# Score rounds and projection halves on 64x64 TensorE tiles, with PV rounds left on 64x32 tiles

## The chip, the cores and the metric

The kernel runs on one core of one Trainium2 chip. The metric is the device time of one execution in microseconds (us); lower is better. Five engines matter: TensorE (PE, with its weight loads listed apart as PEld), VectorE (DVE), ScalarE (ACT), GpSimd (POOL) and SyncE (SP), which issues most DMAs.

## The reference

The reference normalises `x` (2048 rows of 512), runs multi-query attention with 32 heads of width 16 that share one key head and one value head, runs a dense block with SiLU, and joins the two:

```python
xn = _layernorm(x)                                    # [2048, 512]
q = (xn @ wq) in 32 heads of 16;  k = xn @ wk;  v = xn @ wv
p = softmax(q k^T * 16 ** -0.5);  s = (p v) @ wo      # one k, one v for all heads
h = silu(xn @ w1);  g = silu(h @ w2)                  # 512 -> 1792 -> 512
out = x + s * g
```

All tensors are bf16; only `x`, the five weights and `out` are in HBM.

## The kernel before

**Work.** The 2048 queries are cut into 4 chunks of 512 columns, the 32 heads into groups of 4, which makes 32 groups (g) of a chunk and four heads. A *score round* multiplies 64 keys by the queries of two of a group's heads: its result fills one PSUM bank, 128 partitions (64 keys for each head) by 512 queries. There are 2048 score rounds. Their exponentials go two ways. ScalarE takes part of the banks with `Exp` into `pa_sb` (line 1570). VectorE takes the others with a scale and a cast to integers into `db_sb` (line 951), from which GpSimd makes shifted copies in `ds_sb` by integer additions (line 1136). A *PV round* then multiplies such a block by the values (16 value columns and 16 columns of weights that sum the denominator, so 32 wide) and adds it into the group's output bank (line 1214). The exponential that VectorE makes is used in four copies, so there are more PV products than score blocks; one PV round takes two blocks.

**Projections.** `product` (its matmuls are at line 644) cuts every 128-row step of four projections into two halves of 64 rows: `q` (from `wq`), `h` (from `w1`), `z` (from `w2`) and `w` (from `wo`). `tail_half` (its matmul is at line 1421) does the same with the last chunk's `wo` product. So nearly all of TensorE's work is in rounds whose contraction has 64 rows.

**Two lanes.** A matmul carries a tile size (rows by columns of TensorE's array) and a tile position. In the kernel before, score rounds, PV rounds and projection halves all use tiles of 64 rows by 32 columns, four to a round. A round of lane 0 uses the tiles at (0,0), (0,32), (64,64) and (64,96); a round of lane 1 those at (64,0), (64,32), (0,64) and (0,96). Score rounds are always on lane 1, PV rounds always on lane 0, projection halves on either. The rounds of the two lanes touch no tile in common.

**Order.** A planner in the kernel's Python writes the order of every engine's instructions before the program is built. It works with fixed durations: `MM` = 216 ns for one round on a lane, a latency between each two engines, and `SWITCH` = 105 ns when TensorE passes to a round of another mode letter. The letters are "U" for the 64-row rounds, "C" for 128 rows by 32 columns (lines 530, 572, 674), "H" for 128 by 64 (line 609) and "F" for 128 by 128 (lines 546, 1461, 1530). `Planner.tensor` keeps one clock per lane for "U". The order on TensorE is strict; a wait for a semaphore stands ahead of the instruction that needs it.

**Buffers.** Eight PSUM banks hold score blocks, PV outputs and projection results; the planner gives them out as they come free.

Of the kernel before, what the change touches and what calls it, by code (L numbers as in the profile page):

```python
# [15 lines left out]
P = 128  # L16
# [287 lines left out]
def bass_recurrent_scan__grouped_kv_mqa__dense_activation_silu__prompt_kernel(  # L304
# [27 lines left out]
    NQR, NON = 4, 2 * NOC  # L332

    with ExitStack() as es:
        def sb(name, shape, dt):
            return es.enter_context(nc.sbuf_tensor(name, shape, dt))
# [10 lines left out]
        kt_sb = sb("kt_sb", [P, 2, 2, S], BF16)  # L347
# [3 lines left out]
        qt_sb = sb("qt_sb", [P, NQR, NQ], BF16)  # L351
# [6 lines left out]
        on_sb = sb("on_sb", [P, NON, NQ], BF16)  # L358
# [26 lines left out]
        def bank(b):  # L385
            return ps[:, b * 512:(b + 1) * 512]
# [98 lines left out]
        first = (2, 2, 4, 4, 4)  # L485
        a = 0
        for n in first:
            b = a + n
            tiles = range(a, b)
            g = a // 4  # L490
            y, w, h = rstd_sb[:, a:b], var_sb[:, 0, a:b], var_sb[:, 1, a:b]
# [140 lines left out]
        def product(jb, lhs, rhs, needs):  # L632
            n = len(jb.rounds)
            jb.mode, jb.place, jb.rounds = "U", [0, 0], []
            jb.left = 2 * n

            def half(k, l):
                b, first, last = jb.bank, jb.left == 2 * n, jb.left == 1

                def emit(pe):  # L640
                    for j in range(4):
                        r0 = 64 * (j // 2 ^ l)
                        rows = slice(r0, r0 + 64)
                        h = pe.matmul(bank(b)[32 * j:32 * (j + 1), :], lhsT=lhs(k, rows, 32 * j, 32), rhs=rhs(k, rows),  # L644
                                      start=first, stop=last, tile_position=(r0, 32 * j), skip_group_check=True)
                    return h
                return emit
            jb.half, jb.needs, jb.n = half, needs, n
            return
# [220 lines left out]

        def s_half(b, g, i, kb):
            def emit(pe):
                for j in range(4):
                    r0, k0 = 64 * (j // 2 ^ 1), 64 * kb + 32 * (j % 2)
                    h = pe.matmul(bank(b)[32 * j:32 * j + 32, :], lhsT=kt_sb[r0:r0 + 64, g % 2, i, k0:k0 + 32],  # L875
                                  rhs=qt_sb[r0:r0 + 64, g // 2 % NQR, :], start=True, stop=True, tile_position=(r0, 32 * j),
                                  skip_group_check=True)
                return h
            return emit
# [498 lines left out]
        tb = []  # L1378
# [19 lines left out]
        def tail_reads(r, o):  # L1398
            oi = NOC * (NC - 1) + o
            return ["wo", ("on", oi % NON) if o < NOC - 1 else ("on", oi % NON, r // 2)]  # L1400

        def tail_half(l, t):
            if not tail["half"][l]:
                return INF
            r, o = tail["half"][l][0]
            oi = NOC * (NC - 1) + o
            if t2_task.get(oi) is None or t2_task[oi].op is None or tb[r] not in pool_free:
                return INF
            if l == 0 and any(q == r for q, _ in tail["half"][1]):
                return INF  # L1410
            rr = pl.ready(PE, tail_reads(r, o), [("ps", tb[r])] if o == 0 and l == 1 else ())
            if l == 0 and o == 0:
                rr = max(rr, pl.vis(tail["prev"][r], PE))
            if rr > t + 20:
                return rr
            tail["half"][l].pop(0)

            def emit(pe):
                for j in range(4):
                    r0 = 64 * (j // 2 ^ l)  # L1420
                    h = pe.matmul(bank(tb[r])[32 * j:32 * (j + 1), :],  # L1421
                                  lhsT=on_sb[r0:r0 + 64, oi % NON, r * P + 32 * j:r * P + 32 * (j + 1)],
                                  rhs=wo_sb[r0:r0 + 64, o, :], start=o == 0 and l == 1, stop=False,
                                  tile_position=(r0, 32 * j), skip_group_check=True)
                return h
            tail["prev"][r] = pl.tensor("U", l, MM, emit, tail_reads(r, o), [("ps", tb[r])], t,
                                        after=tail["prev"].get(r) if l == 0 and o == 0 else None)
            return True
# [171 lines left out]
        while True:  # L1600
            e = min(ENGINES, key=pl.clk.get)
            seen, r = quiet[e]
            if seen != pl.count or pl.clk[e] >= r:
                r = steps[e]()
# [73 lines left out]
```

## Time and profile before

| What | Value |
|---|---|
| median of two runs | 680.74 us (679.91 to 681.57) |
| the profiled execution: device time | 679.18 us |
| the profiled execution: span, first to last instruction | 677.4 us |
| granted TensorE clock, mean | 0.999 |
| busy: PE, ACT, DVE, POOL | 666.9, 658.7, 634.5, 606.3 us |
| TensorE matmuls, weight loads | 22037, 22038 |
| score rounds (line 875) | 8192 matmuls in 2048 rounds |
| PV rounds (line 1214) | 8800 matmuls |
| projection halves (line 644), tail halves (line 1421) | 4448 and 96 matmuls |

The time of an execution is 1.78 us more than its span. Matmuls are pipelined and the profile models their ends: a matmul of 512 columns has a duration of about 0.38 us, although another can start on the same tile 0.216 us after it. So the busy share of PE says little; the distance between the starts of two rounds says more. In a row of the timeline, "64*32 64x512" means a tile of 64 rows and 32 columns, and a moving operand of 64 partitions by 512 columns. Rows that follow each other on one engine with the same form are merged ("x4"); the times are the first start and the length from there to the last end.

### The profile page before, as it was taken

What the parts mean: (1) busy time and instruction counts of PE and PEld (TensorE: products, weight loads), DVE (VectorE), ACT (ScalarE), POOL (GpSimd) and SP (SyncE); (2) the same over time, 40 slices, a digit from 0 to 9 for tenths busy, and PEclk for the clock granted to TensorE, in tenths of its full rate; (3) what the DMA queues carried; (4) which work ended last, traced back from release to release, by engine and by line L of the source; (5) the groups of instructions that cost most, each with busy time, mean ns of one, the idle gap of its engine ahead of it and who ended that gap; (6) DMA issues with size and microseconds to landing.
All of it is one profiled execution on the core that took longest, in us unless ns stands there. A gap on an engine that the chain in (4) does not pass through costs nothing.

```text
span 677.4 us, 47302 instructions
## 1 busy us (share of the span) xinstructions
PE 666.9 (98%) x22037; PEld 362.0 (53%) x22038; DVE 634.5 (94%) x1150; ACT 658.7 (97%) x1194; POOL 606.3 (90%) x604
## 2 busy tenths in 40 slices
PE   8999999999999999999999999999999999999997
PEld 4445556555455545555655665555555565555542
DVE  8989999999999999999999999999999999999763
ACT  5899999999999999999999999999999999999996
POOL 4038998999999999989999997899999999998993
PEclk9999999999999999999999999999999999999999
DMA  8510000000000010000000100000000001000000
GB/s 298 170 30 4 4 5 5 4 5 4 5 4 20 21 35 5 4 4 5 5 4 4 36 21 20 5 5 5 4 5 4 20 21 35 4 6 4 5 4 33
DMA packets 11732, 14.98 MB, mean 22 GB/s; under 512 B 1808, under 2 KB 10768, under 8 KB 11536
## 3 DMA queue, kind: packets, MB, share of 16 engines
q1 hardware_dynamic: 10928, 10.78, 5.0%
q8 instruction: 172, 2.82, 1.8%
q0 software_dynamic: 320, 0.92, 0.5%
q10 hardware_dynamic: 288, 0.26, 0.1%
q14 instruction: 24, 0.20, 0.1%
HBM read 8.95 MB, written 2.10 MB: 16 GB/s over the span
## 4 chain that ended last, share of the span: by engine, by line
PE 87%; ACT 9%; DVE 2%; issue 1%
PE ps L875 40%; PE ps L1214 26%; PE ps L644 19%; ACT pa_sb L1570 9%; PE ps L1530 1%; PE ps L1421 0%; PE ps L572 0%; DVE kt_sb L590 0%; DVE stats_sb L478 0%; PE ps L546 0%; DVE xn_sb L507 0%; DVE v_sb L618 0%; DVE xnT_sb L557 0%; PE ps L609 0%; ACT t_sb L692 0%
## 5 line engine op out<-in xcount | busy, mean ns | idle before, releaser
L1570 ACT ACTIVATE pa_sb<-ps 128x512 bf16<-128x512 f32 (+1 forms) x1103 | 628.3, 759 | 7.4 <-PE ps L875 6.1
L1136 POOL INT64_ADD ds_sb<-db_sb x588 | 597.0, 1040 | 25.7 <-PE ps L1214 15.8
L875 PE MATMUL ps<-qt_sb,kt_sb 64*32 64x512 bf16 x8192 | 567.1, 379 | 2.8 <-issue 1.3
L951 DVE TENSOR_SCALAR db_sb<-ps 128x512 uint16<-128x512 f32 x784 | 493.0, 682 | 15.6 <-PE ps L875 12.2
L1214 PE MATMUL ps<-ds_sb,v_sb 64*32 64x512 bf16 x4704 | 410.0, 377 | 0.4 <-issue 0.3
L1214 PE MATMUL ps<-pa_sb,v_sb 64*32 64x512 bf16 x2528 | 317.6, 378 | 1.0 <-issue 0.4
L875 PEld LDWEIGHTS ps<-qt_sb,kt_sb 64*32 64x32 bf16 x8192 | 192.9, 90 | 204.4 <-ACT pa_sb L1570 111.3
L1214 PE MATMUL ps<-db_sb,v_sb 64*32 64x512 bf16 x1568 | 184.4, 377 | 0.0
L1214 PEld LDWEIGHTS ps<-ds_sb,v_sb 64*32 64x32 bf16 x4704 | 154.9, 91 | 22.9 <-issue 3.6
L644 PE MATMUL ps<-w_sb,u_sb 64*32 64x512 bf16 x1792 | 138.0, 377 | 0.1
L644 PE MATMUL ps<-xnT_sb,w_sb 64*32 64x512 bf16 x1792 | 136.7, 377 | 0.2
L1214 PEld LDWEIGHTS ps<-pa_sb,v_sb 64*32 64x32 bf16 x2528 | 93.8, 91 | 22.2 <-ACT pa_sb L1570 9.0
L1214 PEld LDWEIGHTS ps<-db_sb,v_sb 64*32 64x32 bf16 x1568 | 56.7, 91 | 7.7 <-issue 0.7
L644 PEld LDWEIGHTS ps<-xnT_sb,w_sb 64*32 64x32 bf16 x1792 | 44.0, 91 | 16.7 <-ACT pa_sb L1570 3.2
L644 PEld LDWEIGHTS ps<-w_sb,u_sb 64*32 64x32 bf16 x1792 | 45.1, 91 | 13.4 <-issue 1.2
L692 ACT ACTIVATE t_sb<-ps 128x512 bf16<-128x512 f32 x72 | 48.7, 676 | 0.0
L693 DVE SCALAR_TENSOR_TENSOR u_sb<-t_sb,ps 128x512 bf16<-128x512 bf16 x56 | 38.0, 679 | 1.8 <-ACT t_sb L692 1.3
L644 PE MATMUL ps<-xnT_sb,wq_sb 64*32 64x512 bf16 x480 | 37.2, 378 | 0.0
L1231 DVE STREAM_TRANSPOSE ps<-ps 128x512 f32<-128x512 f32 (+1 forms) x33 | 23.2, 706 | 12.9 <-PE ps L1214 12.9
L644 PE MATMUL ps<-wo_sb,on_sb 64*32 64x512 bf16 x384 | 29.3, 378 | 0.0
L1260 POOL DMA_DIRECT2D kt_sb<-kt_sb x4 | 2.8, 700 | 26.7 <-DVE mv_sb L482 18.1
L644 PEld LDWEIGHTS ps<-xnT_sb,wq_sb 64*32 64x32 bf16 x480 | 11.9, 91 | 5.6 <-ACT pa_sb L1570 1.0
(72 smaller groups left out, 182.9 us busy)
## 6 DMA issues: line engine op xcount, KB each, us to landing
w_sb<-in_B_w_dram SPq DMA_DIRECT2D x2, 1792.0 KB, 13.9
xr_sb<-in_A_x_dram SPq DMA_DIRECT2D x16, 128.0 KB, 3.3
out_dram<-ob_sb SPq DMA_DIRECT2D x16, 128.0 KB, 1.8
ds_sb<-in_A_x_dram SPq DMA_DIRECT2D x3, 512.0 KB, 7.2
kt_sb<-kt_sb POOLq DMA_DIRECT2D x4, 224.0 KB, 3.3
wq_sb<-in_A_wq_dram SPq DMA_DIRECT2D x1, 512.0 KB, 5.4
wo_sb<-in_A_wo_dram SPq DMA_DIRECT2D x1, 512.0 KB, 16.4
ds_sb<-in_A_x_dram ACTq DMA_DIRECT2D x2, 128.0 KB, 3.1
```

The lines of the kernel that those rows point to most:

```text
L644: h = pe.matmul(bank(b)[32 * j:32 * (j + 1), :], lhsT=lhs(k, rows, 32 * j, 32), rhs=rhs(k, rows), start=first, stop=last, tile_position=(r ...
L692: t1 = Task(AC, 477.0, lambda a: a.activation(t_sb[:, k, :], bank(b), ACT.Tanh, scale=scale), [("ps", b)], [("t", k)], 0)
L693: t2 = Task(DV, T_P, lambda v: v.scalar_tensor_tensor(out=dst, in0=t_sb[:, k, :], scalar=1.0, in1=bank(b), op0=ALU.add, op1=ALU.mult), [(" ...
L875: h = pe.matmul(bank(b)[32 * j:32 * j + 32, :], lhsT=kt_sb[r0:r0 + 64, g % 2, i, k0:k0 + 32], rhs=qt_sb[r0:r0 + 64, g // 2 % NQR, :], star ...
L951: bt.P[k] = pl.add(Task(DV, T_P, lambda v: v.tensor_scalar(db_sb[:, bt.b, k * NQ:(k + 1) * NQ], bank(b), 128.0 * LOG2E, 128.0 * (SHIFT_BET ...
L1136: whole["po"].append(pl.add(Task(PO, T_P64, lambda g: g.int64_add(ds_sb[:, s, :].bitcast(U64), db_sb[:, bt.b, :].bitcast(U64), words), rea ...
L1214: h = pe.matmul(bank(OB)[q:q + 32, :], lhsT=lhs[rows], rhs=rhs[rows], start=s0, stop=s1, tile_position=(64 * l, q), skip_group_check=True)
L1231: t1 = pl.add(Task(DV, (T_TR - 60.0) / parts + 60.0, lambda v, cols=cols: v.transpose(bank(OB)[:, cols], bank(OB)[:, cols]), [("ps", OB)], ...
L1260: kt1[c] = pl.add(Task(PO, T_SWDGE, lambda e: e.dma_start(kt_sb[DH:P, 1, :, cols], kt_sb[0:P - DH, 0, :, cols]), [("kt", k, a) for k in ra ...
L1530: pl.tensor("F", None, T_COLD if n <= N_COLD else MM, lambda pe: pe.matmul(bank(6), lhsT=zer_sb[:, 0:P], rhs=zer_sb[:, :], start=True, sto ...
L1570: op = pl.place(AC, 0.8333 * NQ * n + T_AF, lambda a: a.activation(pa_sb[:, s * NQ:(s + n) * NQ].rearrange("p (b n) -> p b n", n=NQ), ps3[ ...
```

## The change

In three places a loop of four matmuls on tiles of 64 rows by 32 columns becomes a loop of two on tiles of 64 by 64: the projection halves (`product`), the score rounds (`s_half`) and the halves of the last `wo` product (`tail_half`). The two tiles of lane 0 are then at (0,0) and (64,64), those of lane 1 at (64,0) and (0,64); each covers what two tiles of 64x32 covered. PV rounds (`do_pv`) keep four tiles of 64 by 32. Products, banks, operands and results are the same.

```diff
--- a projection half: product()
-                    for j in range(4):
-                        r0 = 64 * (j // 2 ^ l)
+                    for j in range(2):
+                        r0 = 64 * (j ^ l)
                         rows = slice(r0, r0 + 64)
-                        h = pe.matmul(bank(b)[32 * j:32 * (j + 1), :], lhsT=lhs(k, rows, 32 * j, 32), rhs=rhs(k, rows),
-                                      start=first, stop=last, tile_position=(r0, 32 * j), skip_group_check=True)
+                        h = pe.matmul(bank(b)[64 * j:64 * (j + 1), :], lhsT=lhs(k, rows, 64 * j, 64), rhs=rhs(k, rows),
+                                      start=first, stop=last, tile_position=(r0, 64 * j), skip_group_check=True)
--- a score round: s_half()
-                for j in range(4):
-                    r0, k0 = 64 * (j // 2 ^ 1), 64 * kb + 32 * (j % 2)
-                    h = pe.matmul(bank(b)[32 * j:32 * j + 32, :], lhsT=kt_sb[r0:r0 + 64, g % 2, i, k0:k0 + 32],
-                                  rhs=qt_sb[r0:r0 + 64, g // 2 % NQR, :], start=True, stop=True, tile_position=(r0, 32 * j),
+                for j in range(2):
+                    r0 = 64 * (j ^ 1)
+                    h = pe.matmul(bank(b)[64 * j:64 * j + 64, :], lhsT=kt_sb[r0:r0 + 64, g % 2, i, 64 * kb:64 * kb + 64],
+                                  rhs=qt_sb[r0:r0 + 64, g // 2 % NQR, :], start=True, stop=True, tile_position=(r0, 64 * j),
                                   skip_group_check=True)
--- a half of the last wo product: tail_half()
-                for j in range(4):
-                    r0 = 64 * (j // 2 ^ l)
-                    h = pe.matmul(bank(tb[r])[32 * j:32 * (j + 1), :],
-                                  lhsT=on_sb[r0:r0 + 64, oi % NON, r * P + 32 * j:r * P + 32 * (j + 1)],
+                for j in range(2):
+                    r0 = 64 * (j ^ l)
+                    h = pe.matmul(bank(tb[r])[64 * j:64 * (j + 1), :],
+                                  lhsT=on_sb[r0:r0 + 64, oi % NON, r * P + 64 * j:r * P + 64 * (j + 1)],
                                   rhs=wo_sb[r0:r0 + 64, o, :], start=o == 0 and l == 1, stop=False,
-                                  tile_position=(r0, 32 * j), skip_group_check=True)
+                                  tile_position=(r0, 64 * j), skip_group_check=True)
```

The planner's durations and mode letters are not changed: all these rounds are still "U", of 216 ns on one lane. So the order that it writes is the same as before, round for round, on TensorE and instruction for instruction on the other four engines.

## The prediction

> **What bounds the kernel now.** I read the page first, then TensorE's groups of instructions, then its timeline at two places. The page's first part and its chain say that TensorE carries the end:
>
> ```profile
> PE 666.9 (98%) x22037; PEld 362.0 (53%) x22038; DVE 634.5 (94%) x1150; ACT 658.7 (97%) x1194; POOL 606.3 (90%) x604
> ...
> PE 87%; ACT 9%; DVE 2%; issue 1%
> ```
>
> The chain that ended last is 87% matmuls; ACT holds 9% of it, mostly in the last 55 us. But a busy PE is not yet a full one, so I look at how rounds follow each other (timeline of PE near 300 us):
>
> ```profile
> 300.06 0.39 PE L1214 MATMUL ps<-ds_sb,v_sb 64*32 64x512 bf16 x4
> 300.12 0.39 PE L875 MATMUL ps<-qt_sb,kt_sb 64*32 64x512 bf16 x4
> 300.28 0.39 PE L1214 MATMUL ps<-ds_sb,v_sb 64*32 64x512 bf16 x4
> 300.33 0.39 PE L875 MATMUL ps<-qt_sb,kt_sb 64*32 64x512 bf16 x4
> 300.49 0.39 PE L1214 MATMUL ps<-db_sb,v_sb 64*32 64x512 bf16 x4
> ```
>
> PV rounds (L1214) start at 300.06, 300.28, 300.49: one per 0.216 us. Score rounds (L875) start between them, at 300.12 and 300.33. So two rounds, one on each lane, share every 0.216 us. This sharing is what the whole time rests on: 2048 score rounds, 2200 PV rounds, 1112 projection halves and 24 tail halves are 5384 rounds; on two lanes that is 2692 x 0.216 = 581 us, on one lane 1163 us, and the span is 677.4 us.
>
> The second place is near 39 us, where rounds of another tile size (128*32, L572, the key projection) stand among the 64*32 ones:
>
> ```profile
> 39.03 0.40 PE L644 MATMUL ps<-xnT_sb,w_sb 64*32 64x512 bf16 x4
> 39.36 0.40 PE L572 MATMUL ps<-xnT_sb,wke_sb 128*32 128x512 bf16 x4
> 39.69 0.40 PE L1214 MATMUL ps<-pa_sb,v_sb 64*32 64x512 bf16 x4
> 39.70 0.40 PE L875 MATMUL ps<-qt_sb,kt_sb 64*32 64x512 bf16 x4
> 40.03 0.40 PE L572 MATMUL ps<-xnT_sb,wke_sb 128*32 128x512 bf16 x4
> ```
>
> Here a round starts 0.33 us after the one ahead of it, not 0.216: each change of tile size adds 0.11 us, and nothing of the new size starts until then. The PEld rows of that stretch say why:
>
> ```profile
> 39.36 0.10 PEld L572 LDWEIGHTS ps<-xnT_sb,wke_sb 128*32 128x32 bf16 x4 [0.23 <-DVE xnT_sb L557]
> 39.69 0.10 PEld L1214 LDWEIGHTS ps<-pa_sb,v_sb 64*32 64x32 bf16 x4 [0.23 <-issue]
> ```
>
> The weights of the new size are loaded only as its matmuls start; PEld is idle for 0.23 us before, whereas at 300 us weights are loaded while other rounds stream. The timeline has about 30 such changes, all in the first 43 us and the last 7. One of them changes columns alone:
>
> ```profile
> 9.03 0.22 PE L546 MATMUL ps<-ident,xn_sb 128*128 128x128 bf16 x1
> 9.18 0.41 PE L572 MATMUL ps<-xnT_sb,wke_sb 128*32 128x128 bf16 x16
> ```
>
> A matmul of 128 columns is followed in its own size after about 0.056 us (eight transposes take 0.62 us, the last of them 0.22); here it takes 0.15, so 0.09 more, although the rows (128) stay the same.
>
> **What the change does, part by part.**
>
> *Fewer instructions.* 8192 + 4448 + 96 matmuls become half as many, with as many weight loads. A round still streams 512 columns on its lane, 0.216 us, so the streaming is the same. What could be saved is the spread of four starts (about 0.01 us a round) and PEld work of 90 ns each; both lie beside the streaming of the other lane. I cost it at nothing. Without that cover: 3184 x 0.01 = 32 us less on one lane, 16 on two; and if every load were exposed, one of 64 columns (128*64, L609: 113 ns) against 90 ns is 0.023 x 3184 = 73 us more.
>
> *Changes of tile size.* Score rounds and projections are now 64*64, PV rounds 64*32, and the order alternates between them. In the order of the changed program I count 4175 runs of one tile size; 4142 of the borders lie between 64*64 and 64*32 (2074 one way, 2068 the other). Most runs are one round: 1965 of the 64*32 runs and 1943 of the 64*64 ones. Before, the 64*32 rounds formed a few long runs and the program had 32 borders.
>
> The price of such a border is not in this trace: no row has 64*64. Bounds from the nearest rows: if disjoint tiles of two column widths stream together, nothing (or the savings above). If a border acts like the ones at 39 us, the two lanes no longer share time, and each border adds 0.09 to 0.114 us on top. I take 0.11, the row at 39.36 to 39.69, which has the same 512 streamed columns and 64*32 on one side; the column-only border at 9.18 shows that a change of columns is treated like the others.
>
> The Trainium skill, "TensorEngine Tiling (Array Packing)", section Key Properties, says that a change of tiling mode, not merely of tile, drains TensorE; it lists 64x64 and 64x32 as two modes. The rows above agree for the four sizes that they show; none shows these two against each other. By that rule the sum is the one below.
>
> *The sum.* Inside a run rounds still share time by lane. Counting, run by run, the rounds of the busier lane: 2663 of 64*64 (the other 521 lie beside them) and 2217 of 64*32. That is 4880 x 0.216 = 1054 us of streaming. Borders: 4142 x 0.11 = 456 us. What is left: 128-row work with its old borders, about 19 us (86 + 256 + 160 matmuls, whose streams are 8, 2 and 5 us, and 32 x 0.1); waits in the first 48 us, about 12 (48 less 33 of streaming and 3 of borders), into which some of the new work falls, so 8; and the 5.7 us after the last large matmul. Together 1054 + 456 + 19 + 8 + 6 = 1543 us of span, less a little where a pair of matmuls spreads less than four. With the 1.8 us around the span I say **1540 us**. That execution was 679.18 us, 0.2% under the median of 680.74, which makes no difference here.
>
> *Waits elsewhere.* TensorE is so much later that ACT (658.7 us busy), DVE and POOL wait for it everywhere; their order is unchanged, and the waits of score rounds for ACT (111.3 us) disappear beneath it. Nothing else comes late: semaphores stand where they stood.
>
> *Bounds of this case.* With 0.09 a border: 1543 - 83 = 1460. With 0.114, and 0.023 more for each of 2074 loads of 64 columns: 1543 + 17 + 48 = 1608. So 1450 to 1610.
>
> **Rivals.**
>
> 1. *No drain between 64*64 and 64*32.* The two sizes have the same 64 rows, and score and PV tiles have no place in common; at every border in this trace the new tiles overlap the old. If the array lets disjoint tiles of both widths run, the picture at 300 us stays and the time is 665 to 690, about 678; this is the side that is not slower. The point is whether the next L875 starts before L1214 has streamed. The same section of the Trainium skill says that tiles operate independently; by that sentence alone the time would be this rival's. For it: no row excludes it. Against: the column-only border, and the late weight loads, which also show where loads within a size do overlap. More than 2% faster is unlikely even so: ACT is busy 658.7 us and is not relieved. Chance 14% (11 within 2%, 3 faster).
>
> 2. *Lanes lost, but no border price.* Weights are loaded ahead across a border, only streams don't overlap: 1054 + 19 + 14 = 1087, say 1090. Against it: PEld idle 0.23 us at each border. Chance 5%.
>
> 3. *Partial sharing.* Streams overlap, but a load waits for the border, so that a score and a PV round take 0.31 instead of 0.216: 677 + 2068 x 0.094 = 871. Chance 2%.
>
> 4. *The clock falls.* With TensorE streaming two thirds of the time, the granted clock could fall below 1; at half the streaming takes 2108 and the time is near 2600. Against: the clock was 1.00 from 14 to 20 us, with PE busy 4.53 of 6 us. Chance 1%.
>
> **How the numbers follow.** The forecast of a drain at each border has 78%; some 96% of that lies in its 1450 to 1610, or 75%. With rival 2 that is 80%, so the range is 1080 to 1610. Slower by over 2%: 78 + 5 + 2 + 1 = 86%; within 2% (about what a measurement of this kernel can tell from no change): 11%; faster: 3%.
>
> **What would show it.** In the changed profile, L875 has 4096 matmuls on 64*64. If I am right: near the middle of the span rounds of L875 and L1214 start about 0.32 us after each other, never within one another's stream; PEld loads weights of one size only after the other's matmuls; the chain is nearly all PE; ACT, DVE and POOL are busy about 43%, 41% and 39% of the span; the clock stays near 1. If rounds alternate at 0.216 us, rival 2 holds; if both start within each 0.216 us, rival 1. I'm wrong in size if a border between two widths of the same 64 rows is cheaper than one between row counts, or dearer because of the 64-column load.

## The result, and the profile after

The changed kernel takes 1560.97 us (median of 1560.69 and 1561.24) against 680.74 us before: 2.293 times as long, 95% interval 2.281 to 2.305. The profiled execution took 1561.24 us, its span is 1559.4 us. The forecast was 1540 us.

The page of the changed kernel, first part, clock and chain:

```profile
span 1559.4 us, 34567 instructions
...
PE 1552.6 (100%) x15670; PEld 501.8 (32%) x15670; DVE 690.0 (44%) x1150; ACT 748.0 (48%) x1194; POOL 618.6 (40%) x604
...
PEclk9999999999999999999999999999999999999999
...
PE 98%; DMA 1%; DVE 0%; SPq 0%; issue 0%; ACT 0%
PE ps L1214 45%; PE ps L875 39%; PE ps L644 14%; DMA ds_sb<-in_A_x_dram 0%; DMA kt_sb<-kt_sb 0%; PE ps L1421 0%; PE ps L609 0%; PE ps L572 0%; DVE stats_sb L478 0%; PE ps L546 0%; SPq L399 0%; DVE kt_sb L590 0%; DVE ps L745 0%; DVE fin_sb L734 0%; DVE fin_sb L731 0%
```

TensorE has fewer matmuls (15670 instead of 22037) and is nearly the whole chain, 98%. The other engines have more than half of the span free. The clock never falls.

Two lines of its groups, and the same two before:

```profile
L875 PE MATMUL ps<-qt_sb,kt_sb 64*64 64x512 bf16 x4096 | 746.9, 395 | 0.8 <-DMA kt_sb<-kt_sb 0.4
L1214 PE MATMUL ps<-ds_sb,v_sb 64*32 64x512 bf16 x4704 | 602.3, 386 | 0.0
```

```profile
L875 PE MATMUL ps<-qt_sb,kt_sb 64*32 64x512 bf16 x8192 | 567.1, 379 | 2.8 <-issue 1.3 <-ACT pa_sb L1570 0.9
L1214 PE MATMUL ps<-ds_sb,v_sb 64*32 64x512 bf16 x4704 | 410.0, 377 | 0.4 <-issue 0.3
```

A matmul's own duration hardly moved: 395 and 386 ns instead of 379 and 377. Whoever reads only this column misses the change. It is seen in the starts. The timeline of PE in the middle of the span (start, length, what):

```profile
699.94 0.40 PE L875 MATMUL ps<-qt_sb,kt_sb 64*64 64x512 bf16 x2
700.27 0.40 PE L1214 MATMUL ps<-db_sb,v_sb 64*32 64x512 bf16 x4
700.60 0.40 PE L875 MATMUL ps<-qt_sb,kt_sb 64*64 64x512 bf16 x2
700.93 0.40 PE L1214 MATMUL ps<-db_sb,v_sb 64*32 64x512 bf16 x4
701.26 0.40 PE L644 MATMUL ps<-w_sb,u_sb 64*64 64x512 bf16 x2
701.59 0.40 PE L1214 MATMUL ps<-pa_sb,v_sb 64*32 64x512 bf16 x4
```

One round every 0.33 us, where two rounds shared 0.216 us before. (Below, a run of rounds is a stretch of one tile size, a border is the place where the size changes, and a lone round is one that is a run by itself.) The weight loads of the same stretch:

```profile
700.27 0.10 PEld L1214 LDWEIGHTS ps<-db_sb,v_sb 64*32 64x32 bf16 x4 [0.23 <-issue]
700.60 0.10 PEld L875 LDWEIGHTS ps<-qt_sb,kt_sb 64*64 64x64 bf16 x2 [0.23 <-issue]
...
701.92 0.11 PEld L875 LDWEIGHTS ps<-qt_sb,kt_sb 64*64 64x64 bf16 x2 [0.23 <-ACT pa_sb L1570]
```

Each load starts with its round, after 0.23 us of idle time. The profile puts the last of the three down to ACT, the others to "issue"; the idle time is the same. In the list of waits this looks as follows (total, times, longest):

```profile
PEld ps L1214 <- issue: 483.6, 2041, 0.4
PEld ps L875 <- issue: 241.6, 1018, 0.7
...
PEld ps L875 <- ACT pa_sb L1570: 70.8, 289, 0.5
```

483.6 / 2041, 241.6 / 1018 and 70.8 / 289 are all 0.24 us. It is one wait under several names, and the engine named is not its cause: of 3865 lone rounds a single one is followed later than 0.345 us after its start, whatever name the wait has.

**Where the 882 us of span come from** (1559.4 less 677.4), by the order of the two programs:

| Term | before | after | difference |
|---|---|---|---|
| streaming, busier lane, run by run (0.2158 us a round of 512 columns) | 620.6 | 1069.1 | +448 |
| borders between 64x64 and 64x32: 2068 of 0.117 us, 2074 of 0.110 | 0 | 470 | +470 |
| old borders and waits (what is left) | 56.8 | 20.3 | -37 |

The two prices are measured in the trace: the median distance from the first matmul of a lone round to the first matmul of the next round is 0.333 us after a round of 64x64 and 0.326 us after one of 64x32, less 0.216 of streaming.

### The profile page after: what moved, and what is told of

Same layout as the page of the kernel before. It is cut to its first block, busy times and chain, and to the rows that moved or that the text cites. A ratio compares the mean times of both kernels' runs of the same rounds, so it can differ in the third digit from the quotient of the medians.

```text
span 1559.4 us, 34567 instructions
## 1 busy us (share of the span) xinstructions
PE 1552.6 (100%) x15670; PEld 501.8 (32%) x15670; DVE 690.0 (44%) x1150; ACT 748.0 (48%) x1194; POOL 618.6 (40%) x604
## 4 chain that ended last, share of the span: by engine, by line
PE 98%; DMA 1%; DVE 0%; SPq 0%; issue 0%; ACT 0%
PE ps L1214 45%; PE ps L875 39%; PE ps L644 14%; DMA ds_sb<-in_A_x_dram 0%; DMA kt_sb<-kt_sb 0%; PE ps L1421 0%; PE ps L609 0%; PE ps L572 0%; DVE stats_sb L478 0%; PE ps L546 0%; SPq L399 0%; DVE kt_sb L590 0%; DVE ps L745 0%; DVE fin_sb L734 0%; DVE fin_sb L731 0%
## 5 line engine op out<-in xcount | busy, mean ns | idle before, releaser
L1570 ACT ACTIVATE pa_sb<-ps 128x512 bf16<-128x512 f32 (+1 forms) x1103 | 705.4, 662 | 767.6 <-PE ps L875 758.1
L951 DVE TENSOR_SCALAR db_sb<-ps 128x512 uint16<-128x512 f32 x784 | 534.8, 690 | 796.2 <-PE ps L875 791.3
L875 PE MATMUL ps<-qt_sb,kt_sb 64*64 64x512 bf16 x4096 | 746.9, 395 | 0.8 <-DMA kt_sb<-kt_sb 0.4
L1214 PE MATMUL ps<-ds_sb,v_sb 64*32 64x512 bf16 x4704 | 602.3, 386 | 0.0
L1214 PE MATMUL ps<-pa_sb,v_sb 64*32 64x512 bf16 x2528 | 361.6, 386 | 0.0
L875 PEld LDWEIGHTS ps<-qt_sb,kt_sb 64*64 64x64 bf16 x4096 | 209.4, 104 | 405.9 <-issue 241.6
L644 PE MATMUL ps<-xnT_sb,w_sb 64*64 64x512 bf16 x896 | 144.9, 390 | 0.0
L644 PE MATMUL ps<-w_sb,u_sb 64*64 64x512 bf16 x896 | 140.9, 388 | 0.0
L644 PEld LDWEIGHTS ps<-w_sb,u_sb 64*64 64x64 bf16 x896 | 46.1, 105 | 55.3 <-issue 46.2
L644 PEld LDWEIGHTS ps<-xnT_sb,w_sb 64*64 64x64 bf16 x896 | 43.0, 104 | 52.3 <-issue 39.6
```

The source lines that it names most:

```text
L644: h = pe.matmul(bank(b)[64 * j:64 * (j + 1), :], lhsT=lhs(k, rows, 64 * j, 64), rhs=rhs(k, rows), start=first, stop=last, tile_position=(r ...
L875: h = pe.matmul(bank(b)[64 * j:64 * j + 64, :], lhsT=kt_sb[r0:r0 + 64, g % 2, i, 64 * kb:64 * kb + 64], rhs=qt_sb[r0:r0 + 64, g // 2 % NQR ...
L951: bt.P[k] = pl.add(Task(DV, T_P, lambda v: v.tensor_scalar(db_sb[:, bt.b, k * NQ:(k + 1) * NQ], bank(b), 128.0 * LOG2E, 128.0 * (SHIFT_BET ...
L1214: h = pe.matmul(bank(OB)[q:q + 32, :], lhsT=lhs[rows], rhs=rhs[rows], start=s0, stop=s1, tile_position=(64 * l, q), skip_group_check=True)
L1570: op = pl.place(AC, 0.8333 * NQ * n + T_AF, lambda a: a.activation(pa_sb[:, s * NQ:(s + n) * NQ].rearrange("p (b n) -> p b n", n=NQ), ps3[ ...
```

## The experiments

The theory is that a border between two tile sizes empties TensorE: no round of the new size shares time with one of the old, and there is a price on top. Rival A is that 64x64 rounds are slow by themselves. Rival B is that lanes are lost at a border but no price is paid. All runs are single executions; in the three sets of runs the kernel before took 688.77, 676.52 and 684.68 us beside them. The changed kernel's 1560.97 us is from another set, so a difference of some 12 us between sets says nothing by itself.

| Run | streaming, us | borders 64x64 / 64x32 | expected, us | measured, us |
|---|---|---|---|---|
| scores alone on 64x64 | 1060 | 3983 | 1534 | 1531.84 |
| projections alone on 64x64 | 821 | 1953 | 1065 | 1068.25 |
| all on 64x64, half the PV products | 625 | 0 | 685 | 674.23 |
| changed kernel, half the PV products | 1069 | 4142 | 1545 to 1565 | 1546.95 |
| all on 64x32, scores on PV's lane | 1056 | 0 | 1078 | 1075.59 |
| changed kernel, turns of two | 1040 | 2129 | 1305 to 1350 | 1337.13 |
| changed kernel, turns of four | 1052 | 1085 | 1200 to 1260 | 1229.12 |
| all on 64x64, all PV products | 1093 | 0 | 1115 | 1120.37 |
| changed kernel, scores on PV's tiles | 1164 | 4142 | 1656 | 1653.02 |

### Each half of the change alone

The three loops can be changed one by one. First the scores alone:

```diff
 product(), tail_half(): as before the change, four tiles of 64x32
 s_half(): as after the change, two tiles of 64x64
```

> The changed kernel with only the score rounds on 64x64; projection halves and tail halves are back on 64x32. Counted from its order: 3983 borders between 64x64 and 64x32 (changed kernel 4142), and 1060 us of streaming if rounds share time only inside a run of one tile size. Theory (each border of tile size empties TensorE: no sharing across it, and 0.110 or 0.117 us on top, as measured in the changed kernel): 1060 + 3983 x 0.1135 + 3 (old borders) + 17 (waits, as in the changed kernel) + 2 = 1534 us, 1515 to 1550. Rival A (a round on 64x64 tiles is slow by itself, 0.33 us instead of 0.216, whatever stands beside it): near 700 if the lanes still share, as 2048 x 0.33 = 676. Rival B (the lanes are lost, but a border costs nothing): 1080.

Measured: 1531.84 us. Then the projections alone:

```diff
 product(), tail_half(): as after the change, two tiles of 64x64
 s_half(): as before the change, four tiles of 64x32
```

> The changed kernel with score rounds back on 64x32; only projection and tail halves are on 64x64. Counted from its order: 1953 borders, 821 us of streaming. Theory: 821 + 1953 x 0.1135 + 3 + 17 + 2 = 1065 us, up to 1100 if score rounds wait for ACT again inside the runs of 64x32. Rival A (64x64 rounds slow by themselves): 1136 such rounds on two lanes, so 680 to 740. Rival B: 845.

Measured: 1068.25 us. The scores alone do nearly all of the harm and the projections alone over two fifths of it, so the two do not add up: 1532 - 689 = 843 and 1068 - 689 = 379 us, against 872 for both (1561 - 689). That is how a cost behaves that hangs on borders. If scores already alternate with PV rounds, a projection that joins the scores' size adds few borders (4142 instead of 3983); if scores stay on 64x32, only a projection among them makes borders (1953). Rival A falls with the first run (it gave near 700), as far as the lanes still share; the next runs test 64x64 with sharing. Rival B falls with both.

### All rounds on 64x64, with a control

`do_pv` takes the first block's product alone, on a tile of 64 by 64; the control does the same on 64 by 32:

```diff
-                    for (i, lhs, rhs, s0, s1) in mm:
-                        rows, q = slice(64 * l, 64 * l + 64), 64 * l + 32 * i
-                        h = pe.matmul(bank(OB)[q:q + 32, :], lhsT=lhs[rows], ...
+                    for (i, lhs, rhs, s0, s1) in mm[:1]:
+                        rows, q = slice(64 * l, 64 * l + 64), 64 * l
+                        h = pe.matmul(bank(OB)[q:q + 64, :], lhsT=lhs[rows], ...
 v_lhs():
-            return v_sb[:, j, kb, :]
+            return v_sb[:, j, kb // 2 * 2:kb // 2 * 2 + 2, :].rearrange("p k e -> p (k e)")
```

> All rounds on 64x64 tiles: PV rounds too. Left out: in every PV round the product of the second block, so that a PV round is two matmuls on (0,0) and (64,64); its weights are 64 columns wide, the values of two neighbouring key blocks, so the sums are not the reference's. No border between 64x64 and 64x32 is left (32 old borders), 625 us of streaming against 621 in the kernel before. Theory: the two lanes share again, 670 to 700 us, about 685. Rival A (64x64 is slow by itself): over 900, as 2821 rounds of 0.33 stand on the busier lane. Rival B: as the theory.

> Control for the run with all rounds on 64x64: the changed kernel with the same product left out of each PV round (the second block's), but PV still on 64x32, two matmuls a round. Borders 4142 and streaming 1069 us, both as in the changed kernel. Theory: 1545 to 1565 us, as leaving the product out takes no stream from the lane. Rival: if what costs is the number of matmuls or weight loads, this falls to the time of the run with all rounds on 64x64.

Measured: 674.23 us with PV on 64x64, 1546.95 us with PV on 64x32. The two programs have the same 11310 matmuls and weight loads in the same order; they differ in the column count of the PV tile and its weights. The timeline of PE in the first of them:

```profile
300.25 0.38 PE L1214 MATMUL ps<-pa_sb,v_sb 64*64 64x512 bf16 x2
300.46 0.38 PE L1214 MATMUL ps<-ds_sb,v_sb 64*64 64x512 bf16 x2
300.52 0.40 PE L875 MATMUL ps<-qt_sb,kt_sb 64*64 64x512 bf16 x2
300.68 0.38 PE L1214 MATMUL ps<-ds_sb,v_sb 64*64 64x512 bf16 x2
300.76 0.38 PE L875 MATMUL ps<-qt_sb,kt_sb 64*64 64x512 bf16 x2
300.89 0.38 PE L1214 MATMUL ps<-pa_sb,v_sb 64*64 64x512 bf16 x2
```

The lanes share again, two rounds each 0.216 us. Its weight loads there:

```profile
300.25 0.11 PEld L1214 LDWEIGHTS ps<-ds_sb,v_sb 64*64 64x64 bf16 x2
300.51 0.11 PEld L875 LDWEIGHTS ps<-qt_sb,kt_sb 64*64 64x64 bf16 x2 [0.15 <-DVE db_sb L951]
```

The load for the PV round of 300.46 runs at 300.25, beside the round ahead of it. So 64x64 is not slow in itself, and its dearer load is hidden where the size stays the same. The control is 14 us under the changed kernel; 13 of these are in the starts: a lone PV round of two matmuls ends its 0.326 us some 6 ns sooner, 0.320, and there are 2074 runs of PV rounds.

### The two parts of the loss, apart

In the kernel before, score rounds are put on PV's lane. All tiles stay 64x32, so there is no new border, but nothing is shared between scores and PV:

```diff
 s_half(), before the change:
-                    r0, k0 = 64 * (j // 2 ^ 1), 64 * kb + 32 * (j % 2)
+                    r0, k0 = 64 * (j // 2), 64 * kb + 32 * (j % 2)
```

> The kernel before (all on 64x32, no border of tile size in the long middle) with one edit: score rounds use the tiles of lane 0, where PV rounds are, so the two can't share time. The heads of a score block change places by this, so the sums are not the reference's. Counted: 1056 us of streaming on the busier lane, 32 old borders; the changed kernel has 1069 us and 4142 borders more. Theory: 1056 + 3 + 17 + 2 = 1078 us (1070 to 1110), so that what the changed kernel has over this, 450 to 490 us, is the price of the borders alone, and what this has over the kernel before, about 400 us, is the loss of sharing alone. Rival A (64x64 slow by itself, lanes not lost): the time here says nothing of the change, and the difference should not be 0.11 us a border. Rival B (no border price): this is within 30 us of the changed kernel.

Measured: 1075.59 us. This is 399 us over the kernel before beside it: the loss of sharing. The changed kernel is 485 us over this; 14 of them are its longer streaming (1069.1 against 1055.5), and 471 / 4142 = 0.114 us is the price of a border, from times alone (12 us between sets would be 0.003 of it). The trace's 0.110 and 0.117 have the same mean. Rival B falls here.

### Fewer borders

In `do_pv`, PV rounds become a mode of their own for the planner, so that it costs their borders, and `pe_step` keeps to score rounds and projection halves until n score rounds are placed, then to PV rounds until n are placed (or sooner, if none is ready):

```diff
 do_pv():
-            pl.tensor("U", 0, MM, emit, sorted(reads, key=str), [("ps", OB)], t)
+            pl.tensor("P", None, MM, emit, sorted(reads, key=str), [("ps", OB)], t)
 pe_step():
+            ph, n = st.setdefault("phase", ["S", 0])
+            turn = "PS" if (ph == "S") == (n >= 2) else "SP"
+            for kind in turn:
...
```

> The changed kernel with another order: the planner takes PV rounds as a mode of their own (so it costs their borders) and takes turns of two score rounds, with the projection halves that fit, and two PV rounds. Same products. Counted: 2129 borders between 64x64 and 64x32, 1040 us of streaming. Theory: 1040 + 2129 x 0.1135 + 3 + 20 to 60 of waits + 2 = 1305 to 1350 us. Rival A (64x64 rounds slow by themselves): the order changes nothing, within 3% of 1561. Rival B: 1065 to 1110.

> As the run with turns of two, with turns of four score rounds and four PV rounds: 1085 borders, 1052 us of streaming. Theory: 1052 + 1085 x 0.1135 + 3 + 20 to 80 of waits + 2 = 1200 to 1260 us, so about 0.11 us less for each border that is gone, and above the 1078 of no borders. Rival A: within 3% of 1561. Rival B: as with turns of two, 1075 to 1135.

Measured: 1337.13 us with turns of two, 1229.12 us with turns of four. With another order the changed kernel is 14% and 21% faster, and what goes is mainly the borders: 2013 and 3057 fewer of them are 228 and 347 us at 0.1135. The products are not quite the same, other than the expectations say. In the new order the planner gives VectorE 732 and 748 score blocks instead of 784, and ScalarE the others, whose exponentials need fewer PV products (8488 and 8584 PV matmuls instead of 8800). This is counted in the streaming, which is 29 and 17 us less than the changed kernel's. The timeline of PE with turns of four:

```profile
602.09 1.04 PE L1214 MATMUL ps<-db_sb,v_sb 64*32 64x512 bf16 x16
603.06 1.05 PE L875 MATMUL ps<-qt_sb,kt_sb 64*64 64x512 bf16 x8
```

Four rounds and one border take 603.06 - 602.09 = 0.97 us: 4 x 0.216 and 0.11. Both times lie some 50 us over streaming and borders (1040 + 242 + 5 and 1052 + 123 + 5); that is inside the allowance, but most of it is no wait. The count of streaming takes it that lanes share inside a run, and in ten and twelve long runs of projection halves the rounds of the two lanes stand in blocks, one lane's behind the other's. Such a run with turns of two, in the timeline of PE:

```profile
1261.71 5.40 PE L644 MATMUL ps<-w_sb,u_sb 64*64 64x512 bf16 x56
1267.04 0.61 PE L1214 MATMUL ps<-pa_sb,v_sb 64*32 64x512 bf16 x8
```

Its 28 rounds, 14 of one lane and then 14 of the other, take 1267.04 - 1261.71 = 5.33 us, where 14 x 0.216 is 3.02. These runs are 33 and 28 us over their counted streaming. By these numbers no order brings this kernel back: scores and PV on two sizes don't share, and their 4265 rounds (2048 and 2217) are 920 us at 0.2158 us each, with no border counted. That is an estimate.

### Wasteful, but of one size

The run with all rounds on 64x64, with nothing left out of the PV rounds, so that each streams twice on its two tiles:

```diff
-                    for (i, lhs, rhs, s0, s1) in mm[:1]:
+                    for (i, lhs, rhs, s0, s1) in mm:
```

> All rounds on 64x64, as in the run before with all rounds on 64x64, but nothing left out of the PV rounds: both blocks' products, one after the other on (0,0) and (64,64), 64 weight columns each, so that a PV round streams twice. (The added 32 columns hold a neighbouring key block's values, so the sums are not the reference's; zeros there would take the same time.) Matmuls 15670, as many as the changed kernel; streaming on the busier lane 1093 us against the changed kernel's 1069; 32 borders against 4174. Theory: 1093 + 3 + 17 + 2 = 1115 us (1105 to 1150), 29% under the changed kernel although it streams more. Rival (number of matmuls, or 64-column loads, set the changed kernel's time): within 5% of 1561.

Measured: 1120.37 us. It has as many matmuls as the changed kernel (15670), more 64-column loads and more streaming, and takes 441 us less. So neither the number of matmuls nor the load of 64 columns makes the changed kernel slow. No run has zeros in the added columns.

### Tiles apart or on top of each other

In the changed kernel score tiles and PV tiles have no place in common. Here they have:

```diff
 s_half(), after the change:
-                    r0 = 64 * (j ^ 1)
+                    r0 = 64 * j
```

> The changed kernel with score rounds on lane 0's two tiles of 64x64, (0,0) and (64,64), on top of the PV tiles instead of beside them; the heads of a score block change places by this, so the sums are not the reference's. Borders 4142 as in the changed kernel; streaming 1164 us instead of 1069, because projection halves of lane 0 now queue with scores inside a run. Theory (at a border it makes no difference whether the tiles have a place in common): start to start of a lone round and the next 0.326 and 0.333 us as in the changed kernel, and 1164 + 470 + 3 + 17 + 2 = 1656 us (1640 to 1670). Rival (tiles apart share some of the time across a border): a longer distance at borders than in the changed kernel, and over 1670 us.

Measured: 1653.02 us. The timeline of PE:

```profile
700.47 0.40 PE L875 MATMUL ps<-qt_sb,kt_sb 64*64 64x512 bf16 x2
700.80 0.40 PE L1214 MATMUL ps<-ds_sb,v_sb 64*32 64x512 bf16 x4
701.13 0.40 PE L875 MATMUL ps<-qt_sb,kt_sb 64*64 64x512 bf16 x2
```

The median distance of a lone round and the next is 0.326 and 0.333 us here as well. The 92 us more are 95 us of streaming inside the runs. At a border it makes no difference where the tiles are.

## Why the prediction was right

- **What bounds the kernel.** Right: the sharing of two lanes is what the 677.4 us rested on. The run with scores on PV's lane shows it with no border in the long middle: 399 us. One count is off: there are 2220 PV rounds, not 2200, as 40 of them take a single block; the count run by run has them, so the sum stands.
- **Fewer instructions, costed at nothing.** The size was right, the reason not. With one tile size, 11310 matmuls take 674 us, and the kernel before, with 22037, took 689 beside it and 677 in another set. A gain from fewer instructions, if there is one, can't be told from that spread. But the reason given, that starts and loads lie beside the other lane's streaming, doesn't fit the drain that was forecast: at a lone round there is no such streaming. There the starts do count: their spread is 0.010 us for four matmuls and 0.003 for two. After a lone round of 64x64 0.014 us more than after one of 64x32 is left, which is probably load. Together that makes the 0.007 us by which the border out of 64x64 is dearer, 14 us for 2068 of them.
- **4142 borders that act like those at 39 us.** Right. What the trace before could not show, two column widths on the same 64 rows and on disjoint tiles, acts like the row-count borders. (The lines that the prediction shows have three sizes, not four; the fourth, 128x64, is in the trace before, with 0.316 us from the last matmul of 64x32 to its first.) The rule in "TensorEngine Tiling (Array Packing)" of the Trainium skill, section Key Properties, held for this pair as well (0.33 us from round to round). The sentence beside it, that tiles operate independently, holds here within one size only.
- **The price, 0.11 us.** The main term of the sum that was off: I took 0.11 both ways. It is 0.110 into 64x64 and 0.117 out of it, 470 us instead of 456. That is 14 of the 16 us between the span of 1543 that I summed and the 1559.4, and it is the part of starts and loads that the point on fewer instructions put at nothing. The upper bound allowed for a dearer load of 64 columns (0.023 us each, 48 us in all); the two directions differ by 0.007.
- **Streaming, 1054 us and 16 of 128-row work.** Right: the counted 1069 us, with 20 us for old borders and waits, leave the borders' 470. The run with scores on PV's lane gives 471 for them by another way.
- **Waits elsewhere.** Right in substance. The waits of scores for ACT did not vanish from the list (70.8 us), but they are the border's 0.24 us under another name.
- **Busy shares.** DVE and POOL at 44% and 40% were near the 41% and 39% forecast, ACT at 48% was not at 43%. Its busy time rose from 658.7 to 748.0 us with the same 1194 instructions. Before, exponentials followed each other so closely that their recorded times overlapped (1103 x 759 ns = 837 us in 628.3 us of busy time); after, they stand alone (1103 x 662 ns = 730 us in 705.4). So more of their time is recorded, for the same work.
- **Rivals.** No drain (678 us) is what one tile size gives (674), but not two. No border price (1090) fell to the 471 us over the run with scores on PV's lane. Partial sharing (871) fell to the starts 0.33 us apart, at lone rounds in both directions. The clock stayed at 1.0.

## What to carry to other kernels

Before tiles of another size are put on TensorE, count in the order of its instructions how often the size would change, and which rounds share time now: the cost is the lost sharing plus about 0.11 us a change, and here each of the two is larger than half of the old kernel's time. In this case one tile size throughout was better than the mix, even with more matmuls (680 us, the kernel before) or with some products streamed twice (1120 us against 1561). Look at distances between starts: a matmul's duration, TensorE's busy share and the names in the list of waits said nothing of the drain.

## What the runs showed of the hardware beyond that

The price of a border is the same for runs of one, two and four rounds. From the first matmul of a run to the first of the next, less 0.216 us for each of its rounds, the median is 0.110 us after 64x32 and 0.117 after 64x64 for lone rounds in the changed kernel. With turns of two rounds it is the same, and with turns of four 0.111 and 0.118.

The price has parts. From the last matmul of a run to the first of the next, the median is 0.306 us in both directions where the last round had another of its size ahead of it (so 0.09 over its 0.216 of streaming). The spread of a round's own starts is 0.010 us for four matmuls of 64x32 and 0.003 for two of 64x64. What is left, 0.010 and 0.024 us, stands behind the first round of a run: a lone round is followed 0.316 and 0.330 us after its last matmul, and in the runs with turns the second round comes 0.226 and 0.240 us after the first, the third 0.216 after the second. The difference of 0.014 is near the difference of the two weight loads (104 and 89 ns). I take this for the part of the load that the first round can't hide, but no run here changed the load alone.

The drain depends neither on where the tiles are (0.326 and 0.333 us with tiles apart and on top of each other) nor, in the trace before, on what changes: rows or columns, the next matmul starts about 0.07 us ahead of the modelled end of the last one, unless it waits for data.

One thing no run separates: in all of these kernels the weights fill their tile, so the borders could hang on the tile size of the instruction or on the width of its weights.
